# Fire-biased attention and routed experts on one core: thresholds and scaled weights in place of per-row slopes in the bias layer

## The chip, the cores and the metric

The kernel runs on one core of one Trainium2 chip. The metric is the device time of one execution in microseconds; lower is better. A core has five engines that run beside each other, each through its own instructions in order: PE (TensorE, matmuls), DVE (VectorE), ACT (ScalarE), POOL (GpSimd) and SP (SyncE, which here only issues DMAs). DMAs issued by SP and by POOL run on the same 16 DMA engines, from two queues: q1 is SP's, q0 is POOL's.

## The reference

```python
def _attn_ref(q, k, v, w1, b1, w2):            # B, H, S, D = 8, 8, 576, 64; 32 hidden units
    scores = scale * np.matmul(q, k.transpose(0, 1, 3, 2))
    rel = (pos[:, None] - pos[None, :]).astype(np.float32)
    psi_rel = np.log1p(np.abs(rel))
    psi_i = np.log1p(np.maximum(pos[:, None].astype(np.float32), 1.0))
    x = (psi_rel / psi_i)[..., None]
    h = np.maximum(x @ w1 + b1, 0.0)
    bias = h @ w2                              # S x S x H, the same for every batch
    scores = scores + bias.transpose(2, 0, 1)[None, :, :, :]
    ...                                        # softmax over keys, then times v
def _moe_ref(x, domain_id, w1, w2):            # N, D, E, F = 4608, 512, 8, 1024
    for e in range(E):
        mask = domain_id == e
        h = np.maximum(x[mask] @ w1[e], 0.0)
        out[mask] = h @ w2[e]
```

The attention's output, one row of 512 a token, is the experts' input.

## The kernel before, in words

The program has three stages: a bias phase, the attention over eight batches, and the experts. The bias depends on positions alone, so it is computed once, as exp(bias), and multiplied into the exponentials of every batch.

**Bias phase** (`_phase_bias`). Query positions are done in nine blocks of 64 (`ib`), each in 16 steps (`k16`). A step handles four query positions: the 128 partitions are 4 positions by 32 hidden units. `hidden(ib)` makes one row `hr` [128, 576] a step, the hidden layer of these four positions for all 576 keys, out of a table `L4` of log(1+|distance|), read at an offset that depends on the position. Three rows of a block (five in the first two) run on ACT, as Relu(slope * L + b1), the others on DVE, as max(slope * L, -b1); `slope` is w1/psi of the position, one value a partition. What DVE's form leaves out, +b1, is the same for all keys of a head and falls out of the softmax. `outputs(ib)` then has PE multiply each row, as the stationary operand, by the second layer's weights `W2BIG` [128, 32], block-diagonal with w2 four times, into PSUM tiles `eb` (three buffers), and ACT takes them out with Exp into `biasM` and `biasR` (DVE copies one part raw, `biasW`). The order on PE, DVE and ACT is the order of the program text: the rows of block ib+1 are written ahead of the outputs of block ib. There are 34 row buffers, so rows run at most some two blocks ahead of PE. Between the rows DVE also does the steps of the routing (`next(route)`).

**Start** (`_setup_constants`). POOL makes the integer tables, ACT takes Abs and Ln of them, DVE makes the slopes: those of the first 16 rows first, the rest after row 7 of block 0. Small loads of w1, b1, w2 go by SP.

**Loads.** `_Attention.start` issues on POOL, for batch 0 and then for batch 1: q, k, v (512 KB each as stored, in `load_qk` and `load_v`), the last 64 positions of q and k (`load_last`, four loads into tile `last`), and those of v (`load_vrag`). `last` is first zeroed by a DMA from SP (out of the tile `zero`), as are two of the three `vrag` tiles copied from the first. PE transposes `last` of batch 0 (`at.transposes(0, 4)`) and its first q and k (`at.transposes(0, 0)`) after the outputs of block 4, ahead of those of block 5.

**Sorted rows.** The attention scatters its rows, by expert, into the DRAM tensor `fire_x` of 9216 slots. Slots that no token takes must hold zeros and an index out of bounds, so the whole tensor (9252 KB) is filled ahead of the first scatter: one DMA on SP, behind block 1's outputs (L277), from a tile `zero` that is read 18 times.

**Attention and experts** are the same before and after. In the attention each score tile goes PE, ACT (Exp), DVE (times exp(bias)), PE (times v).

Of the kernel before, what the change touches and what calls it, by code (L numbers as in the profile page):

```python
# [8 lines left out]
F32 = mybir.dt.float32  # L10
# [6 lines left out]
P = 128  # L17
# [27 lines left out]
RAW = {3: 6}  # L45
HEAD = 3
# [55 lines left out]

class _Issue:
# [25 lines left out]
def _setup_constants(tc, G, w1, b1, w2):  # L129
# [10 lines left out]
    nc.sync.dma_start(out=w1col, in_=bass.AP(tensor=w1.tensor, offset=0, ap=[[0, 4], [1, 32], [1, 1]]))  # L140
    G.pb1 = cst.tile([P, 1], F32, tag="pb1", name="pb1")
    nc.sync.dma_start(out=G.pb1, in_=bass.AP(tensor=b1.tensor, offset=0, ap=[[0, 4], [1, 32], [1, 1]]))
    nc.scalar.preload_act_table_set("natural_log_exp_and_others")
    w2f = cst.tile([P, 32], F32, tag="w2f", name="w2f")
    nc.vector.memset(w2f, 0.0)
    for g in range(4):
        nc.sync.dma_start(out=w2f[32 * g: 32 * g + 32, 8 * g: 8 * g + 8], in_=w2[:, :])
    li = G.tmp.tile([P, W4], I32, tag="li", name="li")
    nc.gpsimd.iota(li, base=-C4, channel_multiplier=0, pattern=[[1, W4]])
# [4 lines left out]
    li1 = G.bsb.tile([P, W1], I32, tag="li1", name="li1")  # L154
    nc.gpsimd.iota(li1, base=-(C1 + 512), channel_multiplier=0, pattern=[[1, W1]])
# [4 lines left out]
    for i, f in ((2, -4.0), (1, 4.0), (3, -1.0)):  # L160
        nc.vector.tensor_scalar(out=gs[:, i: i + 1], in0=gs[:, 0:1], scalar1=f, scalar2=None, op0=AO.mult)
    nc.vector.memset(G.zero, 0.0)
    lf = G.tmp.tile([P, W4], F32, tag="lf", name="lf")
    lf1 = li1.bitcast(F32)
    G.L4 = G.bsb.tile([P, W4 + W1], F16, tag="L4", name="L4")
    G.slope = G.bsb.tile([P, NGR], F32, tag="slope", name="slope")

    nc.scalar.activation(out=lf, in_=li, func=AF.Abs, bias=gs[:, 2:3], scale=1.0)
# [11 lines left out]
    G.slopes = slopes  # L180
    slopes(0, 16)
    G.nb1 = cst.tile([P, 1], F32, tag="nb1", name="nb1")
    nc.vector.tensor_scalar(out=G.nb1, in0=G.pb1, scalar1=-1.0, scalar2=None, op0=AO.mult)
    G.W2BIG = G.bsb.tile([P, 32], F16, tag="W2BIG", name="W2BIG")

    def second_layer():
        nc.vector.tensor_scalar(out=G.W2BIG, in0=w2f, scalar1=8.0, scalar2=None, op0=AO.mult)  # L187
    G.second_layer = second_layer

    def last_table():  # L190
        nc.scalar.activation(out=lf1, in_=li1, func=AF.Abs, bias=gs[:, 3:4], scale=1.0)
        nc.scalar.activation(out=G.L4[:, W4:], in_=lf1, func=AF.Ln, bias=1.0, scale=1.0)
# [5 lines left out]
def _phase_bias(tc, G, route, at, x_dram):  # L198
# [837 lines left out]
```

## Time and profile before

| | |
|---|---|
| median of 3 runs | 359.82 us (358.91 to 360.64) |
| profiled execution, its own time | 357.82 us |
| its span in the profile | 356.3 us |
| busy share of the span | PE 91%, DVE 70%, ACT 69%, POOL 46% |
| mean granted TensorE clock | 0.996 of full speed |
| bias phase | from the first row at 5.64 us to the first exponential at 50.01 us on ACT |

The span runs from the first to the last instruction. Idle time of an engine is put down to what ended it ("<-" and the releaser). A timeline row merges instructions of one kind that follow each other; its second number is from the first's start to the last's end, and neighbouring instructions of an engine overlap a little at their ends, so what one costs is read from start to start.

### The profile page before, as it was taken

To read this page: it belongs to the slowest core of one execution; us is meant where nothing else is said; L and a number is where in the kernel's file an instruction comes from. 1 tells how busy PE (TensorE), PEld (TensorE's weight loads), DVE (VectorE), ACT (ScalarE), POOL (GpSimd) and SP (SyncE) were. 2 spreads that over 40 slices of the span, in tenths; PEclk is the share of its full clock that TensorE was granted. 3 is DMA by queue.
4 is the path that set the end of the run, shared out by engine and by line. 5 is a ranking of instruction groups with operands and counts; after the bars stand their busy time and mean duration, and the time that the engine had idled before them with its cause. 6 is when DMAs were issued, how large, how long until landed. Compare 5 with 4: busy or idle time off the path is not lost. (4 is left out here: it accounts for less than half of the span.)

```text
span 356.3 us, 9877 instructions
## 1 busy us (share of the span) xinstructions
PE 325.9 (91%) x4218; PEld 213.7 (60%) x4218; DVE 248.8 (70%) x442; ACT 246.1 (69%) x298; POOL 164.6 (46%) x208
## 2 busy tenths in 40 slices
PE   0489989899999999999998899999999999999993
PEld 0488866666666676666665655555556565555651
DVE  7999999999999999999999851343462526121212
ACT  7999989999999999999999953232314142423230
POOL 8470005617686786858483533405060615041413
PEclk9999999999999999999999999999999999999998
DMA  3999999999999899999999445999999999630302
GB/s 26 217 165 322 365 361 199 198 168 155 169 130 196 109 199 112 196 99 209 143 202 218 109 83 110 320 269 319 292 360 275 362 257 327 115 129 20 125 31 107
DMA packets 89349, 69.20 MB, mean 194 GB/s; under 512 B 43605, under 2 KB 77653, under 8 KB 89304
## 3 DMA queue, kind: packets, MB, share of 16 engines
q0 software_dynamic: 51984, 37.26, 62.3%
q1 hardware_dynamic: 37320, 31.30, 31.3%
q8 instruction: 33, 0.54, 0.6%
q14 instruction: 12, 0.10, 0.1%
HBM read 61.93 MB, written 24.70 MB: 243 GB/s over the span
## 5 line engine op out<-in xcount | busy, mean ns | idle before, releaser
L602 ACT ACTIVATE e<-sc 128x1024 f16<-128x1024 f32 x157 | 148.1, 1059 | 2.1 <-PE sc L573 0.9
L882 ACT ACTIVATE hT<-hps 128x640 f16<-128x640 f32 x56 | 39.4, 704 | 80.6 <-PE hps L846 80.6
L826 POOL DMA_INDIRECT out_dram<-res,ids x40 | 42.7, 1068 | 94.4 <-DVE res L825 77.4
L825 DVE COPY res<-ops 128x512 f32<-128x512 f32 x40 | 27.5, 691 | 73.8 <-PE ops L822 73.8
L613 DVE TENSOR_TENSOR e<-e,biasM 128x2048 f16<-128x2048 f16 x64 | 72.9, 1149 | 1.4 <-ACT e L602 1.3
L822 PE MATMUL ops<-w,hT 128*128 128x512 f16 x320 | 70.9, 379 | 2.2 <-DVE res L825 2.2
L638 PE MATMUL pu<-vext,e 128*128 128x65 f16 (+1 forms) x1280 | 64.8, 194 | 0.0
L846 PE MATMUL hps<-xT,w 128*128 128x320 f16 x448 | 62.0, 299 | 0.0
L638 PEld LDWEIGHTS <-e 128*128 128x128 f16 (+1 forms) x1280 | 56.1, 100 | 8.8 <-issue 6.8
L846 PEld LDWEIGHTS <-w 128*128 128x128 f16 x448 | 43.8, 98 | 18.1
L822 PEld LDWEIGHTS <-hT 128*128 128x128 f16 x320 | 31.1, 98 | 39.0 <-issue 2.7
L573 PE MATMUL sc<-qkT 64*128 64x512 f16 x252 | 50.0, 394 | 3.2 <-ACT e L602 3.2
L680 POOL DMA_INDIRECT fire_x<-xt,posi x32 | 39.7, 1240 | 15.1 <-issue 7.6
L218 DVE TENSOR_SCALAR hr<-L,slope,nb 128x576 f16<-128x576 f16 x113 | 41.4, 431 | 0.1
L636 PE MATMUL pu<-vrag,e 128*128 128x130 f16 (+1 forms) x160 | 35.8, 223 | 1.3 <-DVE xt L652 1.0
L238 PE MATMUL eb<-W2BIG,hr 128*128 128x32 f16 x576 | 24.2, 193 | 13.8 <-DVE W2BIG L187 9.9
L803 DVE CAST w<-st 128x2048 f16<-128x2048 f32 x15 | 18.1, 1225 | 20.5 <-DMA st<-in_moe_w_dram 20.5
L238 PEld LDWEIGHTS <-hr 128*128 128x128 f16 x576 | 21.4, 115 | 17.1 <-POOL vrag L459 6.5
L215 ACT ACTIVATE hr<-L,pb,slope 128x576 f16<-128x576 f16 x31 | 24.6, 875 | 1.2 <-DMA pb<-in_b_dram 1.0
L680 POOL DMA_INDIRECT fire_x<-xl,posi x8 | 9.1, 1133 | 31.3 <-DVE xl L666 12.8
L636 PEld LDWEIGHTS <-e 128*128 128x128 f16 (+1 forms) x160 | 16.0, 100 | 12.5 <-issue 6.6
L652 DVE TENSOR_TENSOR xt<-pu,rz 128x512 f16<-128x512 f32 (+1 forms) x33 | 22.3, 675 | 1.5
(125 smaller groups left out, 349.9 us busy)
## 6 DMA issues: line engine op xcount, KB each, us to landing
st<-in_moe_w_dram SPq DMA_DIRECT2D x15, 1024.0 KB, 9.1
fire_x<-zero SPq DMA_DIRECT2D x1, 9252.0 KB, 37.6
w<-in_moe_w_dram POOLq DMA_DIRECT2D x17, 512.0 KB, 12.6
qn<-in_q_dram POOLq DMA_DIRECT2D x8, 512.0 KB, 7.8
kn<-in_k_dram POOLq DMA_DIRECT2D x8, 512.0 KB, 8.0
vst<-in_v_dram POOLq DMA_DIRECT2D x8, 512.0 KB, 6.8
out_dram<-res,ids POOLq DMA_INDIRECT x40, 6.5
last<-zero SPq DMA_DIRECT2D x2, 256.0 KB
```

The costliest lines, as they stand in the source:

```text
L218: nc.vector.tensor_scalar(out=hr, in0=G.L4[:, c0: c0 + S], scalar1=G.slope[:, m: m + 1], scalar2=G.nb1[:], op0=AO.mult, op1=AO.max)
L238: nc.tensor.matmul(out=eb[:, lj, 32 * k16: 32 * k16 + 32], lhsT=rap(hr, jc, [[4, 128]]), rhs=G.W2BIG[:, 0:32], start=True, stop=True)
L573: mm(out=sc[:, h2, :], lhsT=self.qkT[b, p][hs[h2], 1, 128 * c: 128 * c + 128], rhs=self.qkT[b, p][hs[h2], 0, :], start=not raw, stop=True)
L602: nc.scalar.activation(out=ef[:, 0:n], in_=sf[:, 0:n], func=AF.Exp, bias=0.0, scale=0.125)
L613: self.nc.vector.tensor_tensor(out=job[0], in0=job[0], in1=job[1], op=AO.mult)
L636: mm(out=out, lhsT=last, rhs=vr[:, pair, :], start=True, stop=False, skip_group_check=True)
L638: mm(out=out[:, 65 * h2: 65 * h2 + 65], lhsT=keys[j], rhs=vx[:, 2 * pair + h2, j, :], start=False, stop=(h2 == 1 and j == 3), skip_group_c ...
L680: inst = self.nc.gpsimd.indirect_dma_start(out=self.x_dram[:, :], out_offset=bass.IndirectOffsetOnAxis(ap=self.G.posi[0:n, c:c + 1], axis= ...
L822: nc.tensor.matmul(out=ops_, lhsT=hT[:, fc, t0: t0 + 128], rhs=G.w.w2(e, fc), start=(fc == 0), stop=(fc == 7))
L826: inst = nc.gpsimd.indirect_dma_start(out=out[:], out_offset=bass.IndirectOffsetOnAxis(ap=idx.bitcast(I32), axis=0), in_=res[:], in_offset ...
L846: nc.tensor.matmul(out=hps[:, i, 0:HC], lhsT=G.w.w1(e, dc, fc), rhs=xT[:, dc, HC * hf: HC * hf + HC], start=(dc == 0), stop=(dc == 3))
L882: nc.scalar.activation(out=hT[:, fc, :].rearrange("p (a b) -> p a b", a=2), in_=first(e, xT, ((fc, 0), (fc, 1))), func=AF.Relu, bias=0.0, ...
```

## The change

The hidden row of a position is now taken without its 1/psi: relu(L*w1/psi + b1) is relu(L*w1 + b1*psi)/psi. The table holds L*w1 (`LW`), a row is Relu(LW + b1*psi) on ACT or max(LW, -b1*psi) on DVE, with one pointer operand, the threshold `thr`, and the factor 1/psi goes into the second layer's weights.

- **Weights.** These now differ for every step. DVE forms the products 8*w2/psi (`comp`, 32 steps first, the other 112 after row 6 of block 0), and DMAs on SP (`spread(j)`, four small ones, one for each group of 32 partitions) lay them block-diagonally into one of two zeroed tiles `W2`. A tile serves two blocks of 32 steps in all; tiles 0 and 1 are used in turn (j = 0 to 4), so that a load waits until PE is through with the tile's former content.
- **Rows on ACT** are now 6, 5, 3, 3, 4, 3, 4, 4, 4 in the nine blocks: 36 in place of 31.
- **Start.** The last block's table is taken from the same integers with another bias, its Abs ahead of the rows; DVE scales both tables by w1 and makes two thresholds in place of the slopes' passes. Both memsets of `zero` come at the start.
- **Fill.** `fire_x` is filled by 18 DMAs of 128 rows of 4112 B (526 KB). In blocks 2 to 7 three rows each (steps 0, 6 and 11) hold one back: the DMA is issued when the row is computed.
- **Loads.** POOL's first load of q waits for the first 32 steps' products; what is behind it on POOL follows. SP's DMAs up to the end of the fill are issued in program order (`G.sp_issue`).

SP's queue before, from the start to the transposed load at the attention's end (`dom` are the routing's ids):

```order
L140 DMA w1col<-in_w_dram 128x1x1
L142 DMA pb_88<-in_b_dram 128x1x1
L147 DMA w2f<-in_w_dram 32x8 x4
L301 DMA dom_81<-in_moe_domain_id_dram 128x8x8
L304 DMA dom_81<-in_moe_domain_id_dram 64x8x2
L464 DMA last_153<-zero 128x2x512
L464 DMA last_154<-zero 128x2x512
L461 DMA vrag_146<-vrag_145 128x520
L461 DMA vrag_147<-vrag_145 128x520
L277 DMA fire_x<-zero 2304x1x2056
L998 DMA_TRANSPOSE xA<-fire_x 128x4x512
```

And now, from the routing's ids on:

```order
L218 DMA W_116<-comp 32x256 x4
L499 DMA vrag_155<-vrag_154 128x520
L499 DMA vrag_156<-vrag_154 128x520
L502 DMA last_162<-zero 128x2x512
L502 DMA last_163<-zero 128x2x512
L218 DMA W_117<-comp 32x256 x4
L241 DMA fire_x<-zero 128x2056 x3
L218 DMA W_116<-comp 32x256 x4
L241 DMA fire_x<-zero 128x2056 x6
L218 DMA W_117<-comp 32x256 x4
L241 DMA fire_x<-zero 128x2056 x6
L218 DMA W_116<-comp 32x128 x4
```

The five ring loads (`W_`) stand between the zeroing copies and the pieces of the fill; the last three pieces follow behind the last row shown. A piece behind a ring load is not issued before it.

DVE's start before, up to the second part of the slopes:

```order
L162 MEMSET zero 128x1028
L169 TENSOR_SCALAR slope<-si,gs 128x128
L171 TENSOR_SCALAR slope<-si,gs 128x16
L177 RECIPROCAL slope<-slope 128x16
L178 TENSOR_SCALAR slope<-slope,w1col 128x16
L183 TENSOR_SCALAR nb_123<-pb_88 128x1
L218 TENSOR_SCALAR hr<-L_114,slope,nb_123 128x576 x6
L177 RECIPROCAL slope<-slope 128x128
L178 TENSOR_SCALAR slope<-slope,w1col 128x128
L187 TENSOR_SCALAR W2BIG<-w2f 128x32
```

And now, up to the second part of the products:

```order
L185 MEMSET zero 128x1028
L186 MEMSET zero 128x4
L187 MEMSET W_116 128x512
L189 RECIPROCAL rec<-psi 128x32
L190 MEMSET W_117 128x512
L193 TENSOR_SCALAR LW<-lf,w1col 128x1075
L197 TENSOR_SCALAR thr<-psi,pb_88 128x144 x2
L207 SCALAR_TENSOR_TENSOR comp<-w2c,rec 128x256
L256 TENSOR_SCALAR hr<-LW,thr 128x576 x5
L206 RECIPROCAL rec<-psi 128x112
L207 SCALAR_TENSOR_TENSOR comp<-w2c,rec 128x896
```

The first rows now stand behind the scaled table, the thresholds and the first products; the products' second part stands where the slopes' second part stood.

The diff, cut to its core:

```diff
+ROWS = {3: (3, 8, 13), 4: (2, 6, 10, 14), 5: (2, 5, 8, 11, 14), 6: (1, 4, 7, 9, 12, 15)}
+FILL = (0, 6, 11)
+ROWS = [ROWS[n] for n in (6, 5, 3, 3, 4, 3, 4, 4, 4)]
...
+def _behind(tc, inst, before):
+    tc.add_manual_dep(_ins(inst), before.name, mybir.DependencyInfo(
+        mybir.DependencyClass.Sync, mybir.DependencyReason.DATA), reason="paced")
...
-    def slopes(a, b):
-        nc.vector.reciprocal(out=G.slope[:, a:b], in_=G.slope[:, a:b])
-        nc.vector.tensor_scalar(out=G.slope[:, a:b], in0=G.slope[:, a:b], scalar1=w1col[:], scalar2=None,
-                                op0=AO.mult)
...
+    W2 = [G.asb.tile([P, 2, 512], F16, tag="e", name="W2", bufs=8)
+          .rearrange("p a (b m h) -> p (a b) m h", b=2, h=8) for _ in range(2)]
+    G.W2 = lambda m: W2[m // 32 % 2][:, :, m % 32, :]
...
+    def scaled(src, a, b):
+        nc.vector.tensor_scalar(out=G.LW[:, a:b], in0=src, scalar1=w1col[:], scalar2=None, op0=AO.mult)
+    scaled(lf, 0, W4)
+    G.thr = G.bsb.tile([P, 2, NGR], F32, tag="thr", name="thr")
+    for i, f in ((0, 1.0), (1, -1.0)):
+        nc.vector.tensor_scalar(out=G.thr[:, i, :], in0=psi, scalar1=pb1[:], scalar2=f,
+                                op0=AO.mult, op1=AO.mult)
...
+    def second_layer(i):
+        a, n = 32 * i, comp[i].shape[1]
+        if i:
+            nc.vector.reciprocal(out=rec[:, a: a + n, 0], in_=psi[:, a: a + n])
+        return nc.vector.scalar_tensor_tensor(
+            out=comp[i], in0=w2c.to_broadcast([P, n, 8]), scalar=8.0,
+            in1=rec[:, a: a + n, :].to_broadcast([P, n, 8]), op0=AO.mult, op1=AO.mult)
+    G.products = _ins(second_layer(0))
...
+    def spread(j):
+        src, a = (comp[0], 0) if j == 0 else (comp[1], 32 * j - 32)
+        n = min(32, NGR - 32 * j)
+        for g in range(4):
+            gp = slice(32 * g, 32 * g + 32)
+            sp(nc.sync.dma_start(out=W2[j % 2][gp, g, 0:n, :], in_=src[gp, a: a + n, :]))
...
+        def fill(behind):
+            if parts:
+                _behind(tc, G.sp_issue(nc.sync.dma_start(out=parts.pop(0), in_=G.zero)), behind)
...
-                if k16 in ((2, 5, 8, 11, 14) if ib < 2 else (3, 8, 13)):
-                    nc.scalar.activation(out=hr, in_=G.L4[:, c0: c0 + S], func=AF.Relu,
-                                         bias=G.pb1[:], scale=G.slope[:, m: m + 1])
+                if k16 in ROWS[ib]:
+                    row = nc.scalar.activation(out=hr, in_=G.LW[:, c0: c0 + S], func=AF.Relu,
+                                         bias=G.thr[:, 0, m: m + 1], scale=1.0)
                 else:
-                    nc.vector.tensor_scalar(out=hr, in0=G.L4[:, c0: c0 + S],
-                                            scalar1=G.slope[:, m: m + 1], scalar2=G.nb1[:],
-                                            op0=AO.mult, op1=AO.max)
+                    row = nc.vector.tensor_scalar(out=hr, in0=G.LW[:, c0: c0 + S],
+                                            scalar1=G.thr[:, 1, m: m + 1], scalar2=None, op0=AO.max)
...
+                if ib > 1 and k16 in FILL:
+                    fill(_ins(row))
...
+            if ib in (2, 4, 6):
+                G.spread(ib // 2 + 1)
...
-                nc.sync.dma_start(out=x_dram.rearrange("(p c r) d -> p c (r d)", p=P, r=4),
-                                  in_=G.zero.to_broadcast([P, NSLOT // P // 4, 4 * XW]))
...
+            if not self.nat:
+                _behind(self.tc, inst, self.G.products)
```

## Rows read from the trace of the kernel before

**Rows 1.** Busy time by stretch: PE, PEld, DVE, ACT, POOL; clock, DMA share, GB/s.

```profile
27.10:31.70 4.60, 4.21 (x96) 3.53 (x96) 4.60 (x15) 4.60 (x7) 0.00 (x0) 1.00 1.13 313
...
60.00:100.00 40.00, 38.22 (x646) 25.97 (x645) 39.26 (x60) 38.79 (x44) 24.18 (x33) 1.00 1.16 163
100.00:140.00 40.00, 39.49 (x663) 26.85 (x661) 39.22 (x57) 39.67 (x45) 29.03 (x36) 1.00 1.10 150
```

**Rows 2.** ACT timeline, bias phase: start, us, line, op, tiles, count [idle before].

```profile
25.83 2.41 ACT L215 ACTIVATE hr<-L,pb,slope 128x576 f16<-128x576 f16 x3
28.11 1.96 ACT L256 ACTIVATE biasM<-eb 128x1024 f16<-128x1024 f32 x2
29.92 0.42 ACT L251 ACTIVATE biasR<-eb 128x256 f16<-128x256 f32 x1
...
47.08 2.04 ACT L256 ACTIVATE biasM<-eb 128x1024 f16<-128x1024 f32 x2 [0.91 <-PE eb L238]
...
50.01 2.85 ACT L602 ACTIVATE e<-eb 128x1024 f16<-128x1024 f32 x3 [0.45 <-PE eb L579]
```

**Rows 3.** ACT by line and form, to 60 us: total us, mean ns.

```profile
L168 ACT ACTIVATE lf<-li,gs 128x1075 f32<-128x1075 int32 x1 | 1.2, 1191 | 0.0
L174 ACT ACTIVATE L<-lf 128x1075 f16<-128x1075 f32 x1 | 1.1, 1086 | 0.0
```

**Rows 4.** DVE timeline: work with one pointer, none, two, none.

```profile
9.43 0.29 DVE L178 TENSOR_SCALAR slope<-slope,w1col 128x128 f32<-128x128 f32 x1
9.64 0.17 DVE L187 TENSOR_SCALAR W2BIG<-w2f 128x32 f16<-128x32 f32 x1
...
27.15 4.51 DVE L218 TENSOR_SCALAR hr<-L,slope,nb 128x576 f16<-128x576 f16 x13
...
52.49 0.68 DVE L511 COPY vext<-vst 128x2048 f16<-128x2048 f16 x1
53.10 0.15 DVE L360 TENSOR_SCALAR apref<-apref 128x8 f32<-128x8 f32 x1
```

**Rows 5.** Timeline of the start: SP, POOL, ACT, PE, and SP's fill.

```profile
2.43 1.86 SPq L147 DMA_DIRECT2D w2f<-in_w_dram  x4
...
5.17 1.09 POOL L483 DMA_DIRECT2D qn<-in_q_dram  x1
...
5.64 3.90 ACT L215 ACTIVATE hr<-L,pb,slope 128x576 f16<-128x576 f16 x5 [0.96 <-DMA pb<-in_b_dram]
...
9.87 1.27 PE L238 MATMUL eb<-W2BIG,hr 128*128 128x32 f16 x26 [9.87 <-DVE W2BIG L187]
...
22.41 0.60 SPq L277 DMA_DIRECT2D fire_x<-zero  x1
```

**Rows 6.** DMA issues within 0:30, 7.4:8, 11.4:12.6, 22.8:24 us: KB, us to landing.

```profile
w2f<-in_w_dram SPq DMA_DIRECT2D x4, 1.0 KB, 2.8
...
vst<-in_v_dram POOLq DMA_DIRECT2D x1, 512.0 KB, 13.2
...
last<-in_q_dram POOLq DMA_DIRECT2D x2, 32.0 KB, 8.9
...
last<-in_q_dram POOLq DMA_DIRECT2D x2, 32.0 KB, 23.2
```

**Rows 7.** DMA packets, stretches 16:17, 19:20, 29:32, 41:44, 27:28; packets, MB.

```profile
q0 software_dynamic: 389, 0.19, 142.2%
...
DMA packets 1002, 0.15 MB, mean 154 GB/s; under 512 B 917, under 2 KB 1002, under 8 KB 1002
...
DMA packets 452, 1.06 MB, mean 355 GB/s; under 512 B 0, under 2 KB 224, under 8 KB 451
...
DMA packets 527, 1.13 MB, mean 377 GB/s; under 512 B 258, under 2 KB 263, under 8 KB 526
...
q1 hardware_dynamic: 20, 0.08, 21.6%
```

**Rows 8.** PE timeline: the transposes of batch 0's last rows.

```profile
33.97 1.03 PE L514 MATMUL ptl<-idn,last 128*128 128x128 f16 x8
```

More of the change, by code (lines that the diff above doesn't have):

```diff
@@ L139, in _setup_constants @@
     w1col = cst.tile([P, 1], F32, tag="w1col", name="w1col")
-    nc.sync.dma_start(out=w1col, in_=bass.AP(tensor=w1.tensor, offset=0, ap=[[0, 4], [1, 32], [1, 1]]))
-    G.pb1 = cst.tile([P, 1], F32, tag="pb1", name="pb1")
-    nc.sync.dma_start(out=G.pb1, in_=bass.AP(tensor=b1.tensor, offset=0, ap=[[0, 4], [1, 32], [1, 1]]))
+    sp = G.sp_issue
+    sp(nc.sync.dma_start(out=w1col, in_=bass.AP(tensor=w1.tensor, offset=0, ap=[[0, 4], [1, 32], [1, 1]])))
+    pb1 = cst.tile([P, 1], F32, tag="pb1", name="pb1")
+    sp(nc.sync.dma_start(out=pb1, in_=bass.AP(tensor=b1.tensor, offset=0, ap=[[0, 4], [1, 32], [1, 1]])))
     nc.scalar.preload_act_table_set("natural_log_exp_and_others")
[L144 to L149, printed above, removed]
+    w2c = cst.tile([P, 1, 8], F32, tag="w2c", name="w2c")
+    sp(nc.sync.dma_start(out=w2c, in_=bass.AP(tensor=w2.tensor, offset=0, ap=[[0, 4], [8, 32], [1, 8]])))
     si = G.tmp.tile([P, NGR], I32, tag="si", name="si")
@@ L159, in _setup_constants @@
         nc.vector.memset(gs[32 * g: 32 * g + 32, 0:1], float(g))
-    for i, f in ((2, -4.0), (1, 4.0), (3, -1.0)):
-        nc.vector.tensor_scalar(out=gs[:, i: i + 1], in0=gs[:, 0:1], scalar1=f, scalar2=None, op0=AO.mult)
-    nc.vector.memset(G.zero, 0.0)
[L163 to L168, printed above, removed]
@@ L180, in _setup_constants @@
[L180 to L188, printed above, removed]
+    for i, f, c in ((2, -4.0, 0.0), (1, 4.0, 0.0), (3, -1.0, C4 - C1 - 512)):
+        nc.vector.tensor_scalar(out=gs[:, i: i + 1], in0=gs[:, 0:1], scalar1=f, scalar2=float(c),
+                                op0=AO.mult, op1=AO.add)
@@ new lines, in _setup_constants @@
+    lf = G.tmp.tile([P, W4], F32, tag="lf", name="lf")
+    lf1 = G.asb.tile([P, 4, 512], F16, tag="e2", name="lf1", bufs=5)
+    lf1 = lf1.rearrange("p a i -> p (a i)").bitcast(F32)[:, 0:W1]
+    G.LW = G.bsb.tile([P, W4 + W1], F16, tag="LW", name="LW")
+    psi = G.bsb.tile([P, NGR], F32, tag="psi", name="psi")
+    nc.scalar.activation(out=lf, in_=li, func=AF.Abs, bias=gs[:, 2:3], scale=1.0)
+    nc.vector.tensor_scalar(out=psi[:, 0:128], in0=si[:, 0:128], scalar1=gs[:, 1:2], scalar2=1.0,
+                            op0=AO.add, op1=AO.max)
@@ new lines, in _setup_constants @@
+    nc.vector.tensor_scalar(out=psi[:, 128:], in0=si[:, 128:], scalar1=gs[:, 0:1], scalar2=1.0,
+                            op0=AO.add, op1=AO.max)
+    nc.scalar.activation(out=psi, in_=psi, func=AF.Ln, bias=1.0, scale=1.0)
+    nc.scalar.activation(out=lf, in_=lf, func=AF.Ln, bias=1.0, scale=1.0)
+    nc.scalar.activation(out=lf1, in_=li[:, 0:W1], func=AF.Abs, bias=gs[:, 3:4], scale=1.0)
+    W2 = [G.asb.tile([P, 2, 512], F16, tag="e", name="W2", bufs=8)
+          .rearrange("p a (b m h) -> p (a b) m h", b=2, h=8) for _ in range(2)]
@@ L190, in last_table @@
+    G.products = _ins(second_layer(0))
+    G.second_rest = lambda: second_layer(1)
+    def spread(j):
[4 more added lines that the diff above has]
+            sp(nc.sync.dma_start(out=W2[j % 2][gp, g, 0:n, :], in_=src[gp, a: a + n, :]))
+    G.spread = spread
     def last_table():
-        nc.scalar.activation(out=lf1, in_=li1, func=AF.Abs, bias=gs[:, 3:4], scale=1.0)
@@ L192, in last_table @@
-        nc.scalar.activation(out=G.L4[:, W4:], in_=lf1, func=AF.Ln, bias=1.0, scale=1.0)
+        nc.scalar.activation(out=lf1, in_=lf1, func=AF.Ln, bias=1.0, scale=1.0)
+        scaled(lf1, W4, W4 + W1)
     G.last_table = last_table
@@ L203, in _phase_bias @@
          tc.tile_pool(name="fps", bufs=1, space=bass.MemoryType.PSUM) as fps:
+        x_rows = x_dram.rearrange("(n p r) d -> n p (r d)", p=P, r=4)
+        parts = [x_rows[n] for n in range(NSLOT // P // 4)]
+        def fill(behind):
+            if parts:
+                _behind(tc, G.sp_issue(nc.sync.dma_start(out=parts.pop(0), in_=G.zero)), behind)
         def hidden(ib):
@@ L956 @@
     x_dram = nc.dram_tensor("fire_x", (NSLOT, XW), F16, kind="Internal").ap()
-    G.issue = _Issue(tc)
+    G.issue, G.sp_issue = _Issue(tc), _Issue(tc)
     G.w = _Weights(G, nc, moe_w1, moe_w2)
```

55 lines of the change are left out of this document (29 added, 26 removed).

## The prediction

> **What bounds the kernel now.** I read the table by stretches first, then the timelines of ACT, DVE and PE, then the DMA queues. In a block of the bias phase ACT and DVE are both busy for the whole 4.60 us, PE for 4.21; later, in the attention, ACT is busy 39.67 of 40 us [rows 1]. So from 5.6 us until the attention ends, what ACT loses or saves in the bias phase should move the end one for one: this is where the change has to be priced. The phase ends for ACT at 50.01, with the first exponential [rows 2].
>
> **ACT, the clean sum.** In the ACT timeline a block is three rows (25.83 to 28.11, 0.76 each), two biasM (to 29.92) and one biasR [rows 2]. A row reads two pointers, scale and bias. What one costs shows at two calls of the same width: Abs with a pointer bias 1191 ns, Ln with constants 1086 [rows 3]. So 0.10 us a pointer, and a new row about 0.66.
> - 31 rows lose a pointer: -3.1. Five rows come over from DVE (36 in `ROWS`): 5 x 0.66 = +3.3.
> - The Abs of the last block's table (about 0.8, by its 636 columns to the 1075 of rows 3) moves ahead of the first row, where ACT waits anyway (0.96, for b1) [rows 5]: -0.8.
> - The first row now needs the scaled table and the thresholds from DVE. The DVE work ahead of it, by rows of like size (one-pointer f32 work of 128 columns: 0.21 from start to start [rows 4]), ends at 6.0 to 6.9 us, against 5.64 before [rows 5]; I take 6.5: +0.9.
> - ACT's waits at the end, behind DVE's late rows (0.91 and 0.45 [rows 2]), go if DVE gets ahead: -1.4.
>
> That is -3.1 + 3.3 - 0.8 + 0.9 - 1.4 = -1.1. ACT is 0.88 us less busy from 60 to 100 than from 100 to 140 [rows 1]; DVE's lead (next part) should save most of it, -0.7: **-1.8 clean**.
>
> **DVE, the cover for that.** Rows start 0.347 us apart (4.51 us for 13). A copy of 2048 f16 without a pointer takes 0.61 to the next start, so a column costs 0.30 ns at most, and 576 of them 0.17: 0.175 of a row is fixed, its two pointers in it. One-pointer work of 128 f32 columns takes 0.21, less 128 columns at twice that rate 0.13 fixed, 0.04 under the row's [rows 4]. So one pointer is worth between 0 and half the fixed part (0.09); I take 0.055, near the 0.04: a row of 0.29. 108 x 0.29 = 31.3 against 113 x 0.347 = 39.2: -7.9. Added: the second block of products (896 columns, about 1.1 as for 1075 on ACT [rows 3]), a scaled last table (636 columns, 0.5), a start 1.3 later; removed: the slopes' two passes (about 0.5). DVE ends its rows some 5 us earlier and stops being a bound. [...]
>
> **The first ring load** waits for the first products, at about 7.2. Four issues took 1.86 on SP [rows 5], a small load 2.8 from issue to landing [rows 6]: it lands at 11.6 to 12.5. Before, PE began at 9.87 [rows 5]; but ACT has eleven rows ahead of its first eviction (6.5 + 7.3 = 13.8), and 32 matmuls take about 1.1: nothing on the path up to 12.6. Bounds: 0, and +5 if it took the 8.9 us of a load behind others [rows 6]; I take 0, since these pieces go out ahead of the loads. PE matmuls themselves keep their shape: 0.
>
> **The queues, where I expect the loss.** The fill moves from one issue at 22.4 us, after most early loads were in, to 18 pieces of 128 packets that follow rows from about 16.5 us on; and POOL's loads, which went out from 5.17 on, now wait for the products: 2.1 us later [rows 5]. The two collide.
> - While both queues have work, they take turns: of 452 packets from 29 to 32 us 224 are the loads' (under 2 KB), the rest the fill's; from 41 to 44 us 258 of 527 are small ones of the loads [rows 7]. So loads get 75 packets of 512 B a microsecond, or 86 small ones. Alone they got 389, and 1002 where most were small [rows 7].
> - A fill piece takes 128/75 = 1.7 us there. Three are tied to each block, and a block takes ACT about 4.4: 1.45 us each. Once running, the fills leave the DMA engines no pause.
> - What waits: batch 0's q, k, v (3 x 1024 packets), then its `last` rows (4 x 256 packets of 128 B). Before, v was issued at 7.5 and took 13.2, and `last` went out at 11.4 and took 8.9 [rows 6]: both in at about 21, ahead of the fill. That fill beside batch 1's loads stretched the same kind of load to 23.2 [rows 6].
> - Now: by 18.5, when the first piece's data should flow (issue plus some 2 us), the loads stand where they stood at about 16.0 before (2.1 later, 0.4 for the ring loads): 3.5 us short of the last packet (v in at 20.7, less some 1.2 for the landing), x 389 = 1,360 packets of q, k, v left, then 1,024 small ones.
> - Without a pause these would need 18 + 12 us; but the pieces behind the last ring load can't go before PE is through, so the engines come free at 18.5 + 15 x 1.7 = 44 and `last` lands at about 46. The first pieces follow DVE's rows through the routing steps and wait for a ring load, so I expect about 3 us of pauses: 3 x 389 = 1,170 packets, the other 190 in 2.5 us, then 12 for the small ones and about 1.5 to landing: 18.5 + 19 = **37.5**. With 5 us of pauses they are in by 32.5 and nobody waits.
>
> Who waits: PE, in order, has the transposes of `last` between blocks 4 and 5, at 33.97 before [rows 8], about 32.5 in the clean case. Behind them stand block 5's matmuls, and behind those ACT's biasM and DVE's biasW. With about 0.5 of slack, ACT loses 37.5 - 33 = **4.5 us**.
>
> **Sum:** -1.8 + 4.5 = +2.7. The profiled execution was 357.82 us (span 356.3), so 360.5 by its own time. It lies 2.0 under the median of the runs (359.82); on that scale I predict **362.5 us**.
>
> **The rivals.**
> - *The loads come through (faster).* If single pieces start slowly or leave gaps (5 us of pauses in all), `last` is in at 32.5 and the clean sum stands: 359.8 - 1.8 = 358.0, down to 357.3 if ACT's first row starts at 6.0. For it: the big fill, issued at 22.41 [rows 5], had only 20 packets through by 28 [rows 7], and such a start, some 5 us, would save the loads here as well. Against it: the one-for-one turns above, and pieces that queue up once a block is shorter than three of them.
> - *DVE's row does not shrink.* If one pointer costs as much as two, 108 x 0.347 is only 1.7 under before, and the products and the later start eat that: DVE again ends the phase, at about 50. Time 359.5 to 360.5, no change, if the loads hold; the slower rows also give more pauses. Against it: the 0.04 that I read above.
> - *The last ring load is late.* It stands on SP behind fifteen pieces, and can't land before 44 to 50; block 8's matmuls want it at about 49. That costs 0 to 2 us at the end of the phase: 358 to 360 without the first loss, nothing on top of it.
>
> **How the numbers follow.** Late loads with a loss over the clean gain: 0.48, forecast 362.5, own range 360.5 to 367.8 (landing at 43). Clean: 0.30. DVE unchanged or a late ring load alone: 0.22. A measurement can tell 0.5% (1.8 us) from no change. The clean case lies on that line and the extra savings are as likely as not: it gives 0.24 to faster and 0.06 to same; the forecast 0.43 to slower and 0.05 to same; the rest mostly same, with 0.03 each way. So faster 0.27, same 0.27, slower 0.46. The range runs from the clean case to a landing at 43, 357.5 to 367.8; left out are landings near 46 and a gain over 2.3.
>
> **What would show it.** Right: PE idle before the transposes of `last`, released by the load, with ACT idle before block 5's biasM; load packets at 75 a microsecond from about 19; ACT rows at 0.66 and DVE rows at 0.29 from start to start; the first exponential at 52 to 56. Wrong: those transposes with no wait and the first exponential at 48 to 49 (clean), or DVE rows still 0.34 apart. The forecast falls if the fill's packets do not fill the stretch from 19 to 33 us.

## The result, and the profile after

| | before | after |
|---|---|---|
| median on the same chip | 358.85 us (356.33 to 360.64, 11 runs) | 361.07 us (360.01 to 362.31, 11 runs) |
| ratio | | 1.0071, interval 1.0044 to 1.0099 |
| profiled execution, its span | 357.82, 356.3 | 361.04, 359.5 |
| PE's first matmul | 9.87 | 13.90 |
| ACT's first row to its first exponential | 5.64 to 50.01 | 5.94 to 52.47 |

The change makes the kernel 0.7% slower, 2.2 us by the medians; 2.7 were forecast. The first exponential comes 2.46 us later, the second group of them 2.34 later (57.47 against 55.13), and what lies behind is nearly as long as before (307.0 us from the first exponential to the end of the span, 306.3 before). So most of the loss is made in the bias phase: 2.46 us of the 3.2 between these two executions. (Of the runs below, x2 and y1 were profiled in a disturbed execution, where the time is longer; only a wait of 21.7 us is read from the one, and the bias phase from the other.) The timeline of ACT after the change, each stretch behind a wait (columns as in [rows 2], which answer to it):

```profile
5.94 7.43 ACT L253 ACTIVATE hr<-LW,thr 128x576 f16<-128x576 f16 x11 [0.40 <-DVE thr L197]
15.12 2.04 ACT L295 ACTIVATE biasM<-eb 128x1024 f16<-128x1024 f32 x2 [1.75 <-PE eb L277]
30.20 1.02 ACT L295 ACTIVATE biasM<-eb 128x1024 f16<-128x1024 f32 x1 [0.35 <-PE eb L277]
36.24 0.38 ACT L290 ACTIVATE biasR<-eb 128x256 f16<-128x256 f32 x1 [0.88 <-PE eb L282]
49.54 2.04 ACT L295 ACTIVATE biasM<-eb 128x1024 f16<-128x1024 f32 x2 [0.43 <-PE eb L277]
52.47 2.86 ACT L642 ACTIVATE e<-eb 128x1024 f16<-128x1024 f32 x3 [0.45 <-PE eb L619]
```

Eleven rows take 7.43 us, so a row takes 0.67. All of ACT's waits behind them are for PE. How much they are in all shows in ACT's busy time from the first row to the first exponential (the windows view, columns as in [rows 1]), before and after:

```profile
5.64:50.01 44.37, 33.13 (x814) 29.37 (x816) 44.23 (x129) 42.55 (x59) 13.22 (x20) 1.00 1.20 264
```

```profile
5.94:52.47 46.53, 30.02 (x814) 28.00 (x816) 39.80 (x129) 42.61 (x62) 14.05 (x18) 1.00 1.14 269
```

ACT idles 44.37 - 42.55 = 1.82 us before and 3.92 after. The 2.46 are 0.30 (later first row), 0.06 (work) and 2.10 (more waiting). DVE has 4.4 us less to do and now waits for others (its biasW at 41.41 waits 2.38 for ACT's biasM); its rows are 0.286 apart against 0.347 in [rows 4]:

```profile
31.46 3.72 DVE L256 TENSOR_SCALAR hr<-LW,thr 128x576 f16<-128x576 f16 x13
...
41.41 0.29 DVE L299 CAST biasW<-eb 128x128 f16<-128x128 f32 x1 [2.38 <-ACT biasM L295]
```

PE became the late engine. Its timeline:

```profile
13.90 2.19 PE L277 MATMUL eb<-W,hr 128*128 128x32 f16 x64 [13.90 <-DMA W<-comp]
...
22.55 1.34 PE L277 MATMUL eb<-W,hr 128*128 128x32 f16 x37 [0.46 <-issue]
23.81 1.02 PE L282 MATMUL eb<-W,hr 128*64 128x16 f16 x32
25.15 2.42 PE L277 MATMUL eb<-W,hr 128*128 128x32 f16 x59 [0.31 <-ACT biasM L295]
29.84 0.32 PE L277 MATMUL eb<-W,hr 128*128 128x32 f16 x5 [2.27 <-issue]
...
35.87 0.33 PE L282 MATMUL eb<-W,hr 128*64 128x16 f16 x6 [1.79 <-issue]
36.13 1.03 PE L554 MATMUL ptl<-idn,last 128*128 128x128 f16 x8
...
42.36 2.20 PE L277 MATMUL eb<-W,hr 128*128 128x32 f16 x64 [1.09 <-ACT hr L253]
...
48.83 1.69 PE L277 MATMUL eb<-W,hr 128*128 128x32 f16 x48 [1.79 <-DVE hr L256]
```

The transposes of `last` at 36.13 ([rows 8]) wait for nothing: the stall of the forecast isn't there. Instead PE stops for 2.27 us with 59 of 64 matmuls of block 3 done, and for 1.79 with 26 of 32 of block 4's last group. The rows and the weight tile had been in use for many matmuls, so no data can be missing; "issue" is the profile's name for that. The stops have a period: from 22.55 to 29.84 PE does 37 + 32 + 59 = 128 matmuls, from 29.84 to 35.87 127 (some records are missing), from 42.36 to 48.83 128 again. The last two stops bear the names of engines, but fall on the same places. And the list of DMA packets has a queue "q8 instruction" with one packet of 0.02 MB in each such period; in windows of 0.05 us these packets show at 27.45, 33.65, 40.00 and 46.35, each 2.2 to 2.5 us ahead of PE's restart (queue, packets, MB, share of 16 engines):

```profile
q8 instruction: 1, 0.02, 120.6%
q8 instruction: 1, 0.02, 118.5%
q8 instruction: 1, 0.02, 110.8%
q8 instruction: 1, 0.02, 109.9%
```

So PE was waiting for its own instructions, which come as DMA packets, as the loads and the fill do. Over the whole execution of the change q8 has 33 packets, 0.54 MB, for PE's 4218 matmuls and 4218 weight loads: one packet for 128 of each, as from stop to stop. PE waits for them here, 2.27 us at the longest stop.

Before had such stops too: its PE timeline shows 0.80 ahead of 40.16 and 1.01 ahead of 46.35, both put down to DVE's rows, and 128 matmuls apart; its packets show at 31.50, 37.70 and 43.90. But at the second of these stops DVE was as late itself (timelines of PE and DVE):

```profile
40.16 2.10 PE L238 MATMUL eb<-W2BIG,hr 128*128 128x32 f16 x60 [0.80 <-DVE hr L218]
...
46.35 1.70 PE L238 MATMUL eb<-W2BIG,hr 128*128 128x32 f16 x44 [1.01 <-DVE hr L218]
```

```profile
43.60 3.13 DVE L218 TENSOR_SCALAR hr<-L,slope,nb 128x576 f16<-128x576 f16 x9
```

Those nine are the last rows of block 7. The last of them ends at 46.73, 0.4 us after PE has gone on, and PE's first matmul with it starts at 46.79. So without the wait for the packet PE would have come to that row hardly earlier: before lies on both limits at once. In the change DVE's rows of block 7 were done at 46.25, and PE stood until 48.83.

### The profile page after: what moved, and what is told of

It is laid out like the page before. It is cut to its first block, busy times and chain, and to the rows that moved or that the text cites. A ratio compares the mean times of both kernels' runs of the same rounds, so it can differ in the third digit from the quotient of the medians.

```text
span 359.5 us, 9943 instructions
## 1 busy us (share of the span) xinstructions
PE 321.9 (90%) x4218; PEld 212.1 (59%) x4218; DVE 243.9 (68%) x440; ACT 246.8 (69%) x303; POOL 165.6 (46%) x207
## 5 line engine op out<-in xcount | busy, mean ns | idle before, releaser
L277 PE MATMUL eb<-W,hr 128*128 128x32 f16 x576 | 20.9, 191 | 20.6 <-DMA W<-comp 13.9
L256 DVE TENSOR_SCALAR hr<-LW,thr 128x576 f16<-128x576 f16 x108 | 33.2, 377 | 0.0
L277 PEld LDWEIGHTS <-hr 128*128 128x128 f16 x576 | 20.0, 115 | 22.0 <-DVE hr L256 12.2
L253 ACT ACTIVATE hr<-LW,thr 128x576 f16<-128x576 f16 x36 | 24.8, 770 | 0.4 <-DVE thr L197 0.4
L613 PEld LDWEIGHTS <-qkT 64*128 64x128 f16 x256 | 13.6, 93 | 16.6 <-issue 8.4
```

The lines of the kernel that those rows point to most:

```text
L256: row = nc.vector.tensor_scalar(out=hr, in0=G.LW[:, c0: c0 + S], scalar1=G.thr[:, 1, m: m + 1], scalar2=None, op0=AO.max)
L277: nc.tensor.matmul(out=eb[:, lj, 32 * k16: 32 * k16 + 32], lhsT=rap(hr, jc, [[4, 128]]), rhs=W2, start=True, stop=True)
L613: mm(out=sc[:, h2, :], lhsT=self.qkT[b, p][hs[h2], 1, 128 * c: 128 * c + 128], rhs=self.qkT[b, p][hs[h2], 0, :], start=not raw, stop=True)
```

## The experiments

The table gives, where a run's bias phase is read packet by packet, the instruction packets from 20 us on (some from 23) and the first exponential.

| run | PE starts | instruction packets | first exponential | time to before, interval |
|---|---|---|---|---|
| before | 9.87 | 23.05, 31.50, 37.70, 43.90 | 50.01 | |
| after | 13.90 | 20.10, 27.45, 33.65, 40.00, 46.35 | 52.47 | 1.0071 (1.0044 to 1.0099) |
| x1 | 8.15 | 25.70, 31.70, 38.20, 46.60 | 52.61 | 1.0119 (1.0071 to 1.0166) |
| x4 | 14.22 | 20.35, 23.95, 31.25, 34.95, 39.50, 44.85 | 49.69 | |
| x5 | 13.27 | 23.00, 31.85, 38.40, 44.65 | 50.63 | 1.0020 (0.9994 to 1.0046) |
| y1 | 13.79 | 20.10, 24.20, 32.95, 39.30, 45.45 | 51.43 | 1.0085 (1.0052 to 1.0117) |
| y2 | 14.05 | 20.25, 24.00, 32.65, 39.05, 44.95 | 50.90 | 1.0032 (1.0005 to 1.0058) |
| y3 | 8.14 | 20.30, 24.50, 33.20, 40.00, 46.20 | 52.18 | 1.0087 (1.0055 to 1.0119) |
| y4 | 9.78 | 24.55, 31.25, 37.35, 43.55 | 50.13 | 1.0047 (1.0023 to 1.0072) |

### First round: what makes PE late

**x1: DVE writes the first ring tile.**

```diff
-    G.products = _ins(second_layer(0))
+    for g in range(4):
+        gp = slice(32 * g, 32 * g + 32)
+        inst = nc.vector.scalar_tensor_tensor(out=W2[0][gp, g, :, :], in0=w2c[gp]..., in1=rec[gp, 0:32, :]..., ...)
...
-            G.spread(0)
```

> Edit: DVE writes the first ring tile itself (four operations of 32 partitions in place of the first products and the four DMAs behind them). Theory START (PE begins at 13.90 in place of 9.87 because the first ring load lands late, and can't make that up, since the trace of the change shows one instruction packet on queue q8 for every 128 matmuls and at least 6.2 us between them): PE begins at 7.5 to 8.5, ACT's 1.75 us wait ahead of its first biasM goes and PE's later stalls lie in front of work that ACT isn't waiting for; first exponential 48.6 to 50.0 (52.47 less up to the 3.9 us that ACT waited), time 2.5 to 3.5 us below the change. Theory FILL (the fill's pieces delay PE's instruction packets, and these stalls are what ACT loses): PE's stalls of 2.27 and 1.79 us still reach ACT, only the 1.75 goes; first exponential 50.5 to 51.5, time 1 to 2 us below the change. Theory ROWS (five more rows on ACT): first exponential within 0.5 of 52.5.

PE began at 8.15 and ACT's first wait fell from 1.75 to 0.32, but the first exponential came at 52.61 and the time is no better. START's numbers are missed, and so are FILL's; the place that ROWS named was met, but not by ROWS' cause. The gain lasted up to 31.70, where the packet is 1.95 us ahead of the change's. Then PE waited for the ring load of blocks 6 and 7 (the four DMAs that fill a weight tile anew):

```profile
42.53 2.42 PE L283 MATMUL eb<-W,hr 128*128 128x32 f16 x64 [2.99 <-DMA W<-comp]
```

That load's four issues began at 30.80 on SP, behind nine pieces of the fill, and PE could go on 11.7 us later.

**x2: one fill in place of the pieces.** The diff takes out the held pieces and puts before's one DMA behind `last_table()`.

> Edit: the change with its 18 pieces of the fill put back into one DMA behind the outputs of block 1, as before. Theory START: PE still begins at 13.9, its instruction packets still come no closer than 6.2 us, the stalls put down to issue stay within 0.5 us in all; first exponential 52.0 to 52.8, time within 0.7 us of the change. Theory FILL: the stalls of 2.27 and 1.79 us go, first exponential 50.0 to 51.2, time 1.3 to 2.5 us below the change. Theory ROWS: as START.

1.0566 (1.0526 to 1.0607), worse than any theory had it: the ring load of blocks 4 and 5 now stood on SP's queue behind the whole fill, and PE waited 21.7 us for it. So the pieces are what makes a ring possible at all, and the run says nothing on FILL.

**x4: the pieces held back to the last row of block 8.**

```diff
-                if ib > 1 and k16 in FILL:
-                    fill(_ins(row))
+                last_row = _ins(row)
+                if (ib, k16) == (8, 15):
+                    for _ in range(18):
+                        fill(last_row)
```

> Edit: the 18 pieces of the fill are all held back until the last row of block 8, so that from about 25 us on the bias phase has no fill beside it; the scatters of the attention then start later, so only the bias phase is compared. If full DMA engines set the 6.2 us between two instruction packets of PE (FILL, or START with a cause in the load): the packets come closer than 5.7 us where the engines are not full, PE's issue stalls behind 25 us shrink below 1 us in all, and the first exponential comes at 50.5 to 51.5 (the late start of PE, 1.75 us of ACT's waits, remains). If the distance belongs to the fetch itself: 6.2 us and stalls of some 4 us in all stay, first exponential 52.0 to 52.8.

This is the decisive run. ACT waits once, at its first biasM, and then never again; PE's stops shrink to 0.2 and 0.3 us (timelines of ACT and PE):

```profile
15.45 2.05 ACT L297 ACTIVATE biasM<-eb 128x1024 f16<-128x1024 f32 x2 [2.08 <-PE eb L279]
...
49.69 2.98 ACT L644 ACTIVATE e<-eb 128x1024 f16<-128x1024 f32 x3
```

```profile
22.66 1.34 PE L279 MATMUL eb<-W,hr 128*128 128x32 f16 x37 [0.23 <-issue]
...
33.74 0.33 PE L284 MATMUL eb<-W,hr 128*64 128x16 f16 x6 [0.34 <-issue]
```

The packets behind these stops follow 3.6 us (20.35 to 23.95) and 3.7 us (31.25 to 34.95) on the one before, where the runs with the fill show 5.9 to 6.8 from some 31 us on (x1's 8.4 has the ring load in it). 128 matmuls without a stop take about 4.3 us (an estimate: in the change 64 take 2.20 and the 32 of a last group 1.02), so at 3.7 PE hardly waits and at 6.2 it lives on its packets. It is the packet that comes later, and not PE that takes longer over its matmuls: from a restart of PE to the next packet it is 3.8 to 4.9 us in the change (22.55 to 27.45, 29.84 to 33.65 and so on), 1.3 and 1.2 here (22.66 to 23.95, 33.74 to 34.95). The first exponential comes 2.8 us ahead of the change's, better than expected. (The whole run takes 375.43 us, since the scatters of the attention wait for the fill.) ROWS falls with this run: it has the same 36 rows on ACT.

That the DMA engines are busy is not enough for late packets. From 29 to 32 us of x4, around its packet of 31.25, the loads alone keep them busier by the profile's measure than loads and fill do from 32 to 35 us of the change (queue, packets, MB, share of 16 engines):

```profile
q0 software_dynamic: 1160, 0.59, 143.7%
```

```profile
q1 hardware_dynamic: 239, 0.89, 82.2%
q0 software_dynamic: 237, 0.11, 28.4%
```

The fill moves more bytes in fewer and larger packets (0.89 MB in 239, against 0.59 in 1160). Which of these holds the instructions back, its bytes, its packets' size or its queue, no run tells apart.

x4 is also the measure of the clean sum: ACT's own work is 41.66 us, 0.9 below before:

```profile
5.95:49.69 43.74, 30.37 (x813) 28.25 (x814) 39.86 (x129) 41.66 (x63) 13.71 (x18) 0.91 0.82 109
```

**x5: before, with its weights scaled late** (`G.second_layer()` moved from step 7 of block 0 to step 5 of block 1).

> Edit: the kernel before, with the scaling of W2BIG moved on DVE from behind step 7 of block 0 to behind step 5 of block 1, so that PE begins at 13.3 to 14.0 in place of 9.87; nothing else. Theory START: PE can't make the 4 us up; first exponential 51.8 to 53.5 (50.01 plus 2 to 3.5), time 1.8 to 3.3 us above before. Theories FILL and ROWS: ACT has rows of its own to do until 13.57 and loses 1 us at most, which its 0.91 and 0.45 us of later waits take up; first exponential 50.0 to 50.8, time within 0.8 us of before.

PE began at 13.27, ACT waited 0.84 at its first biasM, and the first exponential came 0.62 later; the time can't be told from before's. START falls: PE made up a late start here, since its packet of 23.00 came 3.9 us after the one of 19.10, while only loads were on the engines. From 31.85 on its packets are about as far apart as before's.

### Second round: the ring or the instructions

**y1: five weight tiles, all loaded at the start; y2: the same with one fill as before; y3: y2 with DVE writing the first tile.**

```diff
-          ... for _ in range(2)]
-    G.W2 = lambda m: W2[m // 32 % 2][:, :, m % 32, :]
+          ... for _ in range(5)]
+    G.W2 = lambda m: W2[m // 32][:, :, m % 32, :]
...
-                    G.spread(1)
+                    for j in range(1, 5):
+                        G.spread(j)
```

> Edit: the change with five weight tiles in place of a ring of two, all loaded at the start (the other three zeroed on DVE behind the second products); the 18 pieces of the fill stay. Theory RING (the ring load for blocks 6 and 7 stands behind pieces of the fill on SP's queue, which is what PE waits for ahead of block 6 and what shifts the end): PE's wait ahead of block 6 (1.09) goes, and with it most of the loss; first exponential 50.0 to 51.0, time 1.5 to 2.5 us below the change. Theory FETCH (full DMA engines put at least 6.2 us between two instruction packets of PE, where the run with the fill held back shows 3.6; the pieces fill the engines from 18 us on, so PE can't make up its start at 13.9): the distances stay at 6.2, first exponential 51.7 to 52.7, time within 0.8 us of the change.

51.43, between the two bands, and the time (1.0085) can't be told from the change's. The wait ahead of block 6 that I had put down to the ring is still there without one: 1.34 us ahead of 41.58, 2.3 behind the packet at 39.30, as the change's ended 2.4 behind that at 40.00 (timeline of PE):

```profile
41.58 2.20 PE L282 MATMUL eb<-W,hr 128*128 128x32 f16 x64 [1.34 <-DVE hr L260]
```

So it is an instruction packet's, and RING falls for the change itself. What came earlier is the packet of 24.20, since the sixteen more loads held SP until 26.93 and the fill began only then: the edit moved the fill too, which I had not meant.

> Edit: as y1, and the fill is one DMA behind the outputs of block 1 again. Theory FETCH: the engines are not full of the fill until some 28 us, PE makes up its late start by then, as in the kernel before with late weights; first exponential 49.5 to 50.7, time 357.5 to 359.0, 2 to 3.5 us below the change and 0.5 above to 1 below before. Theory RING: the same as y1 within 0.5 us.

50.90 and 1.0032, the best version with the new layer, 0.4% under the change, though the two intervals overlap. It lies 0.2 us behind FETCH's band. As FETCH expected, the packet of 24.00 came early (the fill began at 26.92) and the late start was partly made up. But it didn't come below before: PE still loses 1.85 us to one packet ahead of 35.12 (from its timeline):

```profile
35.12 0.33 PE L285 MATMUL eb<-W,hr 128*64 128x16 f16 x6 [1.85 <-issue]
```

> Edit: as y2, and DVE writes the first tile itself, so that PE needn't wait for a load at its start. FETCH: PE begins at about 8.2, ACT's 1.75 us wait goes too; first exponential 48.3 to 49.7, time 356.0 to 358.0, below both kernels. If PE's start still doesn't count: as y2. RING: as y1 less up to 1.4.

Missed, 52.18 and 1.0087. PE began at 8.14 but waited 3.35 us for a row of block 0, since DVE did the second products and three memsets ahead of it, and 2.44 for the routing's matmul. An early start of PE is worth nothing while DVE's rows of block 0 are late.

**y4: before, with the fill in pieces.**

```diff
-                nc.sync.dma_start(out=x_dram..., in_=G.zero.to_broadcast(...))
...
+                if ib > 1 and k16 in (0, 6, 11):
+                    fill(_ins(row))
```

> Edit: the kernel before with its fill cut into the 18 held pieces of the change (and the index words of the tile of zeros set at the start), nothing else. FETCH: instruction packets 6 to 6.5 us apart from 18 us on; PE begins at 9.87 here, some 4 us ahead, so part of that is lead: first exponential 50.3 to 51.5, time 0.3 to 1.5 us above before. RING: no ring load here, first exponential 49.8 to 50.3, time within 0.4 us of before.

The first exponential, 50.13, is at before's place, just under FETCH's band and in RING's. The pieces ran from 17.19 on, and the packet of 24.55 comes 1.5 us later than before's 23.05; but PE, which began at 9.78, had that much in hand, and from 31.25 on its packets come 0.25 to 0.35 us ahead of before's. It ends no earlier for that, because here PE goes from row to row with DVE (44 matmuls in 2.38 us, 1.70 in before):

```profile
45.80 2.38 PE L258 MATMUL eb<-W2BIG,hr 128*128 128x32 f16 x44 [0.35 <-DVE hr L236]
```

So the early pieces cost the bias phase nothing where PE isn't late already. The runs' time is 0.5% up, though, 1.7 us; the profiled execution, the fastest of the twelve, doesn't show where, so this stays open.

### Third round: fewer instructions on PE

**z1: the change with half of the last group's matmuls**, so 80 a block for 96, while ACT and DVE do the same work.

```diff
-                            for h2 in range(2):
-                                nc.tensor.matmul(out=eb[64 * h2: 64 * h2 + 64, ...], rhs=W2[:, :, h2::2], ...)
+                            nc.tensor.matmul(out=eb[0:64, ...], rhs=W2[:, :, 0::2], ...)
```

> Edit: the change with 16 matmuls in place of 32 in each block's last group (keys 512 to 575): the even heads' half is computed, the odd heads' bias of these keys is left out (filled with a constant). ACT's and DVE's work stays; PE issues 80 matmuls a block in place of 96. FETCH (PE lives on instruction packets 6.2 us apart, one for 128 matmuls; in every run so far with the fill beside the bias phase the first exponential comes 6.0 us behind the last packet but one of the phase): the 591 matmuls from the stall at 22.55 to the first exponential become 495, 0.75 packets fewer = 4.6 us, and ACT's own work takes over as the bound; first exponential 49.5 to 51.0, time 1.3 to 2.8 us below the change. If PE's late times come from rows, ring loads or ACT alone: first exponential within 0.5 us of 52.5, at best 51.5 where PE's shorter groups (0.5 us a block) show behind the ring load for block 6.

The first exponential hits FETCH's band. ACT waits once more behind its first biasM, for 0.32, and then not up to the first exponential (timeline of ACT):

```profile
15.35 2.04 ACT L294 ACTIVATE biasM<-eb 128x1024 f16<-128x1024 f32 x2 [1.27 <-PE eb L277]
...
43.05 2.04 ACT L294 ACTIVATE biasM<-eb 128x1024 f16<-128x1024 f32 x2 [0.32 <-PE eb L277]
...
50.19 2.83 ACT L641 ACTIVATE e<-eb 128x1024 f16<-128x1024 f32 x3
54.49 2.12 ACT L302 ACTIVATE biasL<-eb 128x512 f16<-128x512 f32 x4 [1.47 <-PE eb L277]
```

That is 2.3 us gained, though the first row started 0.7 late. Yet the time missed its band (1.0104, 1.0064 to 1.0145): the last row above shows where most went. PE waited 2.52 us for the last ring load ahead of block 8, and the exponentials behind biasL started at 57.02, only 0.45 ahead of the change's. The rest lies behind that (304.7 us from there to the end, 302.0 in the change) and isn't explained. Freed of one wait, PE met the next.

**z2: y2 with one matmul a step for the last 64 keys and two ACT operations of 64 partitions; z3: z2 with an early start; w1: five tiles, early start, one matmul in blocks 4 to 7 alone.**

> Edit: y2 (five tiles, one fill) with one matmul a step for the last 64 keys (64 columns by all 32 outputs, taken out by two ACT operations of 64 partitions, one a head of each pair) and ACT's rows back at 31 (5, 5, then 3). FETCH: 144 matmuls fewer, so PE's packets no longer bind; ACT has its work of y2 (42.4 from 5.94 to the first exponential without waits), less 5 x 0.67, plus 8 x 0.27, and its first wait of 1.9; first exponential 48.8 to 49.8, time 1 to 2 us below y2 (0.2 to 1 below before). If packets don't bind: first exponential 50.5 to 51.5 or later, time as y2.

> Edit: z2, and DVE writes the first tile itself, with the second products, the other tiles' zeroing and their loads moved behind step 3 of block 1, so that DVE's rows of block 0 come without a break. FETCH: ACT's first wait (1.9) goes as well; first exponential 47.0 to 48.3, time 1.2 to 2 us below z2, 1.5 to 3 below before. If something else sets the end: as z2, as y3 was as y2 or worse.

> Edit: the change without ring and pieces (five tiles, three of them zeroed on POOL; one fill as before), DVE writes the first tile, the second products and the loads of the other four tiles behind step 1 of block 1, the routing's matmul behind block 1's outputs in place of block 0's, blocks 4 to 7 with one matmul a step for the last 64 keys and two ACT operations (0.5 us more a block, by z2), ACT's rows 6, 5, then 3 (32). FETCH: PE begins at about 8.2 and has 64 matmuls fewer in the packets behind 31 us (half a packet, 3.1 us), so ACT's own work sets the end: y2's 42.4 us less 4 x 0.67 plus 2.0, from 5.94, and some 0.5 of waits: first exponential 47.9 to 49.3, time 0.5 to 2 us below before of the same chip. If the end is set by DVE's start (1.3 us more work ahead of its rows) or by loads, first exponential 50 to 51 and time 0 to 1.5 us above before.

All three missed FETCH's numbers and none beat before: 1.0162 (1.0111 to 1.0213), 1.0096 (1.0062 to 1.0130), 1.0067 (1.0041 to 1.0093), with first exponentials at 50.96, 52.16 and 51.25. In z2 PE did stop waiting for packets, and ACT waited only 2.50 at its first biasM; but its two half operations take 0.78 from start to start where one took 0.28, 4 us in eight blocks, so ACT itself became the bound. (Its packets are 6.15 to 6.65 us apart from 21.55 on, and PE waits for none: with 80 matmuls a block it needs them no sooner. So the distance alone shows no stall; the restart 2.2 to 2.5 us behind a packet does.) In z3 and w1 the routing's matmul held PE (5.97 and 2.52 us), and in w1 the start was late as well (below). Each edit that freed one wait found another of about its size behind it.

## Why the prediction was right, and where it was wrong

The direction, the range and, within 0.5 us, the size were right, and so was the idea that the change's DMA traffic would make PE late and cost more than it gains. But the wait was not the one named: of the +4.5 nothing came, and the -1.8 doesn't show in the change either. That -1.8 + 4.5 lies near the measured 2.2 is chance. (The 362.5 itself is 1.4 above the median; 1.0 of that is before, 358.85 over its eleven runs in place of 359.82 over three.)

- **Rows.** ACT 0.67 (0.66 forecast), DVE 0.286 (0.29). The rival that DVE's row doesn't shrink fell: one pointer and one operation less (the multiplication went with it, and no run has them apart) took 0.061 us off a row. The 0.04 rested on f32 columns at 0.60 ns, twice the f16 rate, which was the author's estimate; in the change a threshold's 144 columns take 0.205 from start to start and the table's 1075 take 0.65, so some 0.48 ns a column and 0.14 fixed, where 0.13 was taken.
- **ACT's clean work.** Rows and Abs were summed to -0.6; x4, without the fill beside it, shows -0.9. In the change itself it is +0.06. In part that is because work whose input comes late overlaps less with what stands ahead of it: such a pair of biasM takes 2.04 us (at 49.54, behind a wait) instead of 1.91 (at 20.01, 0.09 before the work ahead of it ends).
- **First row.** 5.94, not 6.5: +0.30 in place of +0.9.
- **"ACT's waits at the end, behind DVE's late rows ... go if DVE gets ahead: -1.4".** This failed. The rows were late in before, as it says, but PE's instruction packet alone would have kept PE as long, to 0.1 us. DVE got ahead, and 0.43 and 0.45 stayed, behind the packet of 46.35.
- **"DVE's lead ... should save most of it, -0.7", in the attention.** This failed. From the first exponential to the end the profiled execution takes 0.7 us more, not less.
- **"Nothing on the path up to 12.6 ... I take 0"** for the first ring load. Mis-sized, by its landing above all. The four issues began at 6.41 and took 2.52 (1.86 forecast); PE could start 5.0 us after the last of them, at 13.90, where 2.8 from issue to landing had been taken, and ACT waited 1.75. The load didn't go out ahead of the others: POOL's first issue for q was at 6.70, and from 11 to 12.5 us 438 packets of the loads went by and 1 of SP's queue.

```profile
6.41 2.52 SPq L218 DMA_DIRECT2D W<-comp  x4
```

- **The queues, "so `last` lands at about ... 37.5"** and 4.5 us for ACT. This failed. The pieces left pauses, and from 26 to 29 us 1416 packets of the loads went by against 303 of SP's queue, not one for one (shown below). 1329 packets of that stretch are smaller than 512 B, as those of `last` are, and 48 of the next 3 us: `last` was in at about 31, some 6 us ahead of 37.5, and the 4.5 became 0. (The 2 us from issue to data and the 1.2 for v's landing agree with the trace of before: its first load of q, issued at 5.17, has its first packets at 6.9, and packets of 512 B or more, as v's are, come down to 2 or 3 in 0.1 us at 19.5, 1.2 ahead of v's landing at 20.7. The 1.5 for `last` was an estimate.)

```profile
q0 software_dynamic: 1416, 0.24, 100.4%
q1 hardware_dynamic: 303, 0.46, 52.9%
```

- **The rivals.** "The loads come through" is what happened to the loads, but the 358.0 it named did not follow, since it had no price for PE's instructions. "The last ring load is late" was named for block 8; the one that cost most in x1 was that of blocks 6 and 7.

What the runs show in their place: with the fill beside it, PE gets 128 matmuls' instructions every 5.9 to 6.8 us, and goes on 2.2 to 2.5 us behind each packet. From some 31 us on this is a chain, and in the change, x1, x5, y1, y2 and y3 the first exponential lies 5.95 to 6.12 us behind the last packet of the table. In before it does so too (43.90 to 50.01), but there DVE's rows give the same end; y4, with 6.58, is held by the rows alone. The change takes DVE's limit away and leaves the packets', which a faster ACT and DVE can't shorten (x4 and z1, which loosen it, are where ACT's gain shows). What counts then is how late PE enters the chain: before passes the packet at 31.50, the change at 33.65. The change enters late for two reasons that come together: PE started 4 us later, for its first ring load, and it couldn't make that up, since its next packet took 7.35 us with pieces and loads on the engines at once (3.7 to 4.1 in x5, y1 and y2, where the fill began later). Either alone costs the bias phase little: the late start 0.62 us in x5, the early pieces 0.12 in y4. Ring loads behind pieces are next in line (x1, z1). The share of each can't be summed from single edits, since every one removed uncovered another.

Two things stay open. The fill in pieces costs some 0.5% in both pairs of runs that differ by it (y4 to before, and y1's 1.0085 to y2's 1.0032, whose intervals overlap), 1.7 and 1.9 us, of which the first exponential shows 0.1 and 0.5. So pieces may also cost the change something outside the bias phase; its trace shows 0.7 us there, and no run places it. And in z1 and z2 the time is up by 3.7 and 5.8 us over before, with the first exponential 0.2 and 0.9 later: an early end of the bias phase isn't the whole time.

## What to carry to other kernels

When an engine's idle time is put down to "issue", or to a row that should have been there long ago, count its instructions from stop to stop; if the count repeats and the DMA list shows an instruction packet ahead of each restart, the engine may be waiting for its own program (here 128 matmuls from stop to stop, and a packet 2.2 to 2.5 us ahead of a restart). Many short matmuls beside a bulk transfer such as this fill were bound by that, and there fewer instructions (z1) or no fill in that stretch (x4) brought the bias phase's end forward where faster rows had not. And a load on the path doesn't belong on a queue that also carries a bulk transfer: here PE waited 3.0 us for one that stood behind pieces of the fill (x1), and 21.7 for one behind all of it (x2).

## What the runs showed of the hardware that was not expected

- The instruction packets themselves: as close as 3.6 to 3.9 us where only loads ran beside them (x4, x5), 5.9 at the least with the fill (y2), up to the first exponential.
- DVE was slower beside some of POOL's memsets. In w1 POOL zeroed three tiles from 5.04 on, and the two thresholds that take 0.49 us in the change took 1.15 (timelines of POOL and DVE):

```profile
5.04 3.44 POOL L1043 MEMSET W<- 128x1024 f16 x3
```

```profile
5.55 1.15 DVE L197 TENSOR_SCALAR thr<-psi,pb 128x144 f32<-128x144 f32 x2
```

In z1 the scaled table, at 4.91, took 1.45 in place of 0.74 beside a memset of POOL that took 1.80 from 3.98 on. Not all work was slowed: in w1 the same table kept its 0.74, at 4.90, with the memsets beside it from 5.04 on. No run shows the cause.
